# Second projection of a two-layer attention and SwiGLU kernel: order of chunk 2's turn and load, place of the block-diagonal keys, form of one closing down step

## The chip, the cores and the metric

The kernel runs on one core of one Trainium2 chip. The metric is the device time of one execution in microseconds (us). The engines are named as in the profile: PE (TensorE, matrix products), DVE (VectorE), ACT (ScalarE), POOL (GpSimd) and SP (SyncE, which here issues the transfers). PEld is the weight load of PE.

## The reference

Two equal layers over 2048 tokens of 448 features: attention with 16 query heads of 28 and one shared key and value head, then a SwiGLU feed-forward with 1792 inner features. Both are added to the residual, and both see a layer-normed input.

```python
for layer in range(2):          # the reference writes the two out
    h = layernorm(x)
    q = (h @ wq).heads(16)      # 28 wide each
    k, v = h @ wk, h @ wv       # one head for all
    p = softmax(q @ k.T * 28 ** -0.5)
    x = x + (p @ v).merged() @ wo
    h = layernorm(x)
    x = x + (silu(h @ w_gate) * (h @ w_up)) @ w_down
```

## The kernel before

Tokens are worked in four chunks of 512 (`c` = 0 to 3), each of four tiles of 128 rows. Every factor of a product is split into a high and a low part, and a product is the sum of three matmul passes: high by high, high by low, low by high. The residual `xres` stays in SBUF, and each engine runs its instructions in the order in which the program emits them; nothing is reordered. Transfers go through SP's queue in that same order. Tiles from a pool with a fixed number of buffers are handed out again as soon as the last reader is done; which buffer is taken is decided when the program is built.

**Feed-forward.** `unit(gi, c, n)` works one block of 128 inner features (`fc`) on one chunk: gate and up products, the activation on ACT and DVE, its split `hh`, `hl`. The down product of a unit is deferred: `down` (L861) returns it as two steps, which the next unit runs between and behind its own products. Inner blocks go in groups of two (`groups`), the four chunks inside a group. In half rows the partitions 0 to 63 and 64 to 127 work as two independent halves on two of the four down banks each; the second step swaps the pairs. Between the two steps `between` (L339) lets ACT copy one column of each bank (`seen`), so that the halves don't add to one bank at once. `by_tile` (L894) does the same sum with all 128 rows, one bank after the other, and needs no such look; it is used for the second layer's last chunk and for the very first unit of a layer. `accumulate` (L903) then adds the four banks to `xres`: tiles 0 and 1 on DVE (L911), tiles 2 and 3 by an ACT copy into a tile of the `stage` pool (two buffers, L914) and a POOL addition (L915).

**Hand-over.** After the last group of layer 0, `hand_over(c)` (L929) prepares chunk `c` for the second attention's projection: statistics on DVE (L216, L217), the reciprocal deviation on POOL (L223, L224), then for chunks 0 to 2 the steps `turn` (apply the norm on DVE, L230; turn 32x32 squares on DVE, L271; send the result to DRAM in four transfers, L277), `load` (four transfers back into the free query tiles `qstack`, L964 to L967) and `parts` (split: ACT copies L295 and L299, DVE subtractions L296 and L305). They are queued on `self.soon` with a count of units; `unit` counts down and runs what is due, in list order. For chunks 0 and 1 `load` is part of `turn`. For chunk 2 it stands in the projection's plan, and chunk 3 is turned by PE instead (`flip`, L251).

**Projection.** `project` (L499) does one of 16 steps, four per chunk. A step has an entry `plan[n, 0]` ahead of its matmuls and `plan[n, 1]` and `when[n]` behind them. `q` (L521) is its product (L315): 11 matmuls, an ACT cast and an ACT copy of the result (L548, L549), its output to DRAM (`qd`, L550; parts of the keys, `kt`, L553), and for the two steps of a chunk that carry values a DVE transposition (L556) and POOL copies (L559). Steps 0 to 3 put the copy into the same `stage` tiles. `first_keys` (step 2, L408) loads eight keys; `diagonal` (step 3, L412) makes the block-diagonal key tile `kdiag` from them on DVE; `maxima`, behind steps 6, 10 and 14, multiplies it with the queries (L441) and reduces (L443 to L456).

In the last two units of layer 0 (chunk 3, `fc` 12 and 13) and behind them the emitted order is: step 0 and 1; the last unit; then what is due on `self.soon`, in the order of chunk 1's `parts`, step 2, chunk 2's `turn`; step 3; the last down step, its adds and chunk 3's statistics; steps 4 to 15.

Of the kernel before, what the change touches and what calls it, by code (L numbers as in the profile page):

```python
# [23 lines left out]
NC = S // 512  # L24
NG = H // 4
NF = F // P
# [29 lines left out]
def forward(  # L56
# [31 lines left out]
    phase, banks, threes, live, turn = ExitStack(), [], [], set(), {}  # L88
# [114 lines left out]
    def xtile(pool, again=None):  # L203

        return (
            pool.tile([P, 4, 512], F32R, name="xh"),
            pool.tile([P, 3, 512], F32R, name="xl"),
            again,
        )

    def norm_steps(c, pool=pers, twice=True, each=False):

        got = {}

        def stat(t):
            nc.vector.bn_stats(stats[:, 4 * c + t, :], xres[:, 4 * c + t, :])  # L216
            nc.vector.bn_aggr(mv[:, 4 * c + t, :], stats[:, 4 * c + t, :])  # L217

        def scale(t0=0, n=4):
            if "r" not in got:  # L220
                got["r"] = pers.tile([P, 4], F32, name="rstd", bufs=2)
            r = got["r"][:, t0 : t0 + n]
            nc.gpsimd.tensor_scalar(r, mv[:, 4 * c + t0 : 4 * c + t0 + n, 1], 1.0, EPS, ALU.mult, ALU.add)  # L223
            nc.gpsimd.tensor_tensor(r, r, halfn[:, 0:n], ALU.pow)  # L224

        def apply(t):
            if t == 0:
                got["x"] = pool.tile([P, 4, 512], F32, name="xn")
            o, i, r = got["x"][:, t, 0:D], xres[:, 4 * c + t, :], got["r"][:, t : t + 1]
            nc.vector.tensor_scalar(o, i, mv[:, 4 * c + t, 0:1], r, ALU.subtract, ALU.mult)  # L230
            if twice:
                nc.gpsimd.tensor_copy(got["x"][:, t, D:512], o[:, 384:D])

        if each:
            fs = [lambda t=t: (stat(t), scale(t, 1)) for t in range(4)] + [lambda: None]
        else:
            fs = [lambda t=t: stat(t) for t in range(4)] + [scale]
        return fs + [lambda t=t: apply(t) for t in range(4)], got
# [30 lines left out]
    def turn_tile(got, tb, t):  # L269

        nc.vector.transpose(tb[:, :, 32 * t : 32 * t + 32], got["x"][:, t, 0:D].rearrange("p (b w) -> p b w", w=32))  # L271

    def send(tb, raw):

        to = raw.rearrange("(b d) (g n) -> g d b n", d=32, g=4)
        for g in range(4):
            nc.sync.dma_start(to[g], tb[32 * g : 32 * g + 32])  # L277
# [52 lines left out]
    def side_by_side(lower, upper):  # L330

        assert len(lower) == len(upper)
        for two in zip(lower, upper):
            for po, (a, b), start, stop in two:
                nc.tensor.matmul(po, a, b, start=start, stop=stop, skip_group_check=True)  # L335
# [3 lines left out]
    def between(*pos):  # L339

        for i, po in enumerate(pos):
            nc.scalar.copy(seen[:, i : i + 1], po[:, 0:1])  # L342
# [3 lines left out]
    class Attention:  # L346


        def __init__(self, layer):
            self.layer = layer  # L350
            self.squares = (0, 1, 2) if layer else ()
            self.X, self.norms, self.qd = {}, {}, {}
            self.done, self.spare = 0, {}
            self.order = [(c, m) for c in range(NC) for m in (TURN if c < NC - 1 else LAST)]
            self.seen = 0
            self.steps, self.places = [], []
            self.lent, self.plan = None, {}
            self.hi, self.rowsof, self.kt, self.when = {}, {}, {}, {}
            for c in range(NC):
                self.kt[c] = dram.tile([32, 512], F32, name=f"kt{layer}_{c}")  # L360
                self.at(4 * c + 4, lambda c=c: self.key_load(c))
                self.at(4 * c + 7, lambda c=c: self.key_split(c))
            for i in range(3):
                self.at(4 + 3 * i, lambda i=i: self.stack(i))
                self.at(6 + 3 * i, lambda i=i: self.parts(i))
                if not full:
                    self.at((9, 11, 13)[i], lambda i=i: self.rows(i))
            if not full:
                self.at(2, self.first_keys)
                self.at(3, self.diagonal)  # L370
            for i in range(len(GR) if full else 0):
                fs, place = self.max_steps(i)
                if i == 1:
                    fs[KC] = lambda f=fs[KC]: (f(), self.places[0]())
                self.steps += fs
                self.places.append(place)
# [475 lines left out]
    groups = [range(f, min(f + FG, NF)) for f in range(0, NF, FG)]  # L852

    class FeedForward:
# [6 lines left out]
        def down(self, fs, fc, d, hh, hl):  # L861


            _, _, dh, dl = self.W[fc]
            if self.layer == 1 and d is self.dn.get(NC - 1) and fs is groups[-1]:
                return [lambda: self.by_tile(fs, fc, d, ((hh, dh), (hh, dl), (hl, dh))), lambda: None]
            if fc == 0 and d is self.dn[0]:
                return [lambda: self.by_tile(fs, fc, d, ((hh, dh), (hh, dl), (hl, dh))), lambda: None]
            self.flip = 1 - self.flip
            one, two = ((0, 1), (2, 3)) if self.flip else ((2, 3), (0, 1))  # L870

            def step(ts, first):
                lists = []
                for upper, half in enumerate(ts):
                    rs = slice(64 * upper, 64 * upper + 64)
                    lists.append(
                        [
                            (
                                d[t][:, 0:D],
                                (a[rs, P * t : P * t + P], b[rs, :]),  # L880
                                first and fc == fs[0] and z == 0,
                                not first and fc == fs[-1] and z == 2,
                            )
                            for t in half
                            for z, (a, b) in enumerate(((hh, dh), (hh, dl), (hl, dh)))
                        ]
                    )
                side_by_side(*lists)
                if first:
                    between(*d)  # L890

            return [lambda: step((one, two), True), lambda: step((two, one), False)]
# [36 lines left out]
        def hand_over(self, c):  # L929

            a = self.nxt
            fs, got = norm_steps(c, twice=c == NC - 1)
            for f in fs[:5]:
                f()
            a.pool = self.stage

            if c == NC - 1:

                def ready():
                    for f in fs[5:]:  # L940
                        f()
                    a.norms[c] = got

                a.X[c] = xtile(self.xbp)
                a.plan[5, 1] = [ready]
                return
            to = dram.tile([D, 512], F32, name=f"xt1_{c}")
            raw = [q.bitcast(F32)[:, z, :] for q in qts[1:] for z in range(2)]

            def turn():  # L950
                for f in fs[5:]:
                    f()
                pool = (xpool, self.x1p, self.xbp)
                tb = pool[min(c + 1, 2)].tile([P, 4, 512], F32R, name="xh").bitcast(F32)
                tb = tb.rearrange("p a (b n) -> p (a b) n", n=P)[:, 0 : D // 32, :]
                for t in range(4):
                    turn_tile(got, tb, t)
                send(tb, to)
                a.X[c] = xtile(pool[c])
                if c < 2:  # L960
                    load()

            def load():
                nc.sync.dma_start(qts[1].bitcast(F32), to[0:256, :].rearrange("(k p) n -> p k n", p=P))  # L964
                nc.sync.dma_start(raw[2], to[256:384, :])
                for half in (slice(0, 64), slice(64, 128)):
                    nc.sync.dma_start(raw[3][half, :], to[384:448, :])  # L967

            def parts():
                halved(a.X[c], raw, range(4), nc.scalar.copy, nc.vector.tensor_tensor)  # L970

            self.soon.append([1, turn])
            if c == 2:
                a.plan[4, 1] = [load]
                a.plan[7, 0] = [parts]
                return
            self.soon.append([3, parts])
            self.soon.append([4 - c, lambda: [a.project() for _ in range(2 - c)]])
# [164 lines left out]
    fs, got = norm_steps(0)  # L1143
# [23 lines left out]
    for c in range(1, NC):  # L1167
        fs, got = norm_steps(c)
# [39 lines left out]
```

## Time and profile before

| | us |
|---|---|
| median of 3 runs | 1944.67 (1944.64 to 1945.7) |
| profiled execution, device time | 1948.05 |
| its span, first to last instruction | 1946.3 |
| PE busy in the span | 1933.1 |
| DVE, ACT, POOL busy | 978.1, 1256.8, 563.8 |
| mean granted clock of PE | 0.998 |

The second projection lies at about 966 to 1028 us of the span. Lines of a timeline give the start, the duration, engine, line and operation, what is written and read, how many instructions are merged, and in brackets the idle time of the engine ahead of it with the one that ended it. PE's matmuls overlap: a new one starts about every 0.2 us, though each lasts about 0.4.

### The profile page before, as it was taken

To read this page: it belongs to the slowest core of one execution; us is meant where nothing else is said; L and a number is where in the kernel's file an instruction comes from. 1 tells how busy PE (TensorE), PEld (TensorE's weight loads), DVE (VectorE), ACT (ScalarE), POOL (GpSimd) and SP (SyncE) were. 2 spreads that over 40 slices of the span, in tenths; PEclk is the share of its full clock that TensorE was granted. 3 is DMA by queue.
4 is the path that set the end of the run, shared out by engine and by line. 5 is a ranking of instruction groups with operands and counts; after the bars stand their busy time and mean duration, and the time that the engine had idled before them with its cause. 6 is when DMAs were issued, how large, how long until landed. Compare 5 with 4: busy or idle time off the path is not lost. (4 is left out here: it accounts for less than half of the span.)

```text
span 1946.3 us, 43775 instructions
## 1 busy us (share of the span) xinstructions
PE 1933.1 (99%) x18369; PEld 1325.7 (68%) x18369; DVE 978.1 (50%) x1675; ACT 1256.8 (65%) x1863; POOL 563.8 (29%) x608
## 2 busy tenths in 40 slices
PE   9999999999999999999999999999999999999998
PEld 7544544445469999999974445454454799988887
DVE  6655575665754322322665565657656532232223
ACT  4799899898953333333359998989989433333332
POOL 4213123122215333432342221122231352333420
PEclk9999999999999999999999999999999999999999
DMA  5211011021122011100251110110211220011102
GB/s 160 63 33 33 20 32 50 23 54 33 35 81 73 17 33 32 32 19 25 60 156 48 34 34 18 43 38 26 53 52 30 81 61 26 17 32 32 33 2 77
DMA packets 105474, 87.52 MB, mean 45 GB/s; under 512 B 25304, under 2 KB 85464, under 8 KB 105272
## 3 DMA queue, kind: packets, MB, share of 16 engines
q1 hardware_dynamic: 103576, 83.25, 15.4%
q8 instruction: 144, 2.36, 0.5%
q10 hardware_dynamic: 1696, 1.43, 0.2%
q14 instruction: 58, 0.48, 0.1%
HBM read 59.48 MB, written 23.33 MB: 43 GB/s over the span
## 5 line engine op out<-in xcount | busy, mean ns | idle before, releaser
L669 ACT ACTIVATE pt<-three 128x1536 f32<-128x1536 f32 x512 | 722.1, 1478 | 52.9 <-PE three L643 52.8
L703 PE MATMUL bank<-pt,vsb 128*32 128x512 f32 x3072 | 490.8, 598 | 0.6 <-ACT pt L669 0.6
L703 PE MATMUL bank<-pair,vsb 128*32 128x512 f32 x1024 | 487.7, 598 | 0.0
L643 PE MATMUL bank<-qstack,keys 32*128 32x512 f32 x1536 | 472.7, 425 | 0.0
L335 PE MATMUL bank<-xh,wgh 64*128 64x512 f32 x1712 | 439.0, 389 | 0.4 <-ACT seen L342 0.4
L643 PE MATMUL three<-qstack,keys 32*128 32x512 f32 x4608 | 429.0, 408 | 0.5 <-ACT stage L549 0.3
L643 PEld LDWEIGHTS bank<-qstack,keys 32*128 32x128 f32 x1536 | 243.2, 183 | 248.1 <-issue 125.4
L666 DVE COPY pair<-bank 128x512 f32<-128x512 f32 x512 | 353.9, 691 | 96.5 <-PE bank L643 65.6
L335 PE MATMUL bank<-xh,wgl 64*128 64x512 f32 x1391 | 363.8, 390 | 0.0
L335 PE MATMUL bank<-xl,wgh 64*128 64x512 f32 x1284 | 329.5, 389 | 0.0
L1035 DVE TENSOR_TENSOR sg<-bank,sg 128x512 f32<-128x512 f32 x112 | 77.3, 690 | 486.8 <-ACT sg L1034 476.3
L335 PE MATMUL bank<-wdh,h 64*128 64x448 f32 x1728 | 320.8, 363 | 0.8 <-DVE h L1041 0.4
L671 ACT ACTIVATE pair<-pair 128x1024 f32<-128x1024 f32 x254 | 277.6, 1093 | 0.0
L643 PEld LDWEIGHTS three<-qstack,keys 32*128 32x128 f32 x4608 | 262.0, 183 | 14.2 <-DVE xres L614 1.5
L703 PEld LDWEIGHTS bank<-pt,vsb 128*32 128x32 f32 x3072 | 101.7, 109 | 249.2 <-issue 153.2
L335 PEld LDWEIGHTS bank<-xh,wgh 64*128 64x128 f32 x1712 | 260.9, 184 | 15.2 <-issue 1.0
L915 POOL TENSOR_TENSOR xres<-stage,xres 128x448 f32<-128x448 f32 x107 | 126.1, 1197 | 479.9 <-ACT stage L914 479.7
L711 DVE TENSOR_TENSOR o<-bank,o 128x512 f32<-128x512 f32 x224 | 154.7, 691 | 202.1 <-PE bank L703 202.0
L335 PEld LDWEIGHTS bank<-wdh,h 64*128 64x128 f32 x1728 | 238.4, 184 | 12.4 <-DVE h L1041 1.2
L342 ACT COPY seen<-bank 128x1 f32<-128x1 f32 x646 | 79.4, 163 | 244.7 <-PE bank L335 242.0
L335 PEld LDWEIGHTS bank<-xh,wgl 64*128 64x128 f32 x1391 | 214.9, 184 | 12.6
L335 PE MATMUL bank<-wdl,h 64*128 64x448 f32 x864 | 212.0, 366 | 0.0
(150 smaller groups left out, 2133.2 us busy)
## 6 DMA issues: line engine op xcount, KB each, us to landing
o<-rd SPq DMA_DIRECT2D x32, 256.0 KB
qraw<-qd SPq DMA_DIRECT2D x128, 56.0 KB
xt<-tb SPq DMA_DIRECT2D x32, 224.0 KB
wdr<-in_B_w_down_dram SPq DMA_DIRECT2D x28, 224.0 KB
xn<-xt SPq DMA_DIRECT2D x8, 768.0 KB
wr<-in_B_w_gate_dram SPq DMA_DIRECT2D x28, 192.0 KB
wr<-in_B_w_up_dram SPq DMA_DIRECT2D x28, 192.0 KB
qd<-stage SPq DMA_DIRECT2D x20, 224.0 KB
```

The source lines that it names most:

```text
L335: nc.tensor.matmul(po, a, b, start=start, stop=stop, skip_group_check=True)
L342: nc.scalar.copy(seen[:, i : i + 1], po[:, 0:1])
L643: nc.tensor.matmul(three[:, j, :] if j < 3 else one, k[js, kp, ks], q[js, part, :], start=(z == 0), stop=(z == 2), tile_position=(32 * j, 0),)
L666: copies.append(nc.vector.tensor_copy(pt1, one))
L669: es.append(nc.scalar.activation(pt, threes[y], AF.Exp, scale=SCALE))
L671: es.append(nc.scalar.activation(pair, pair, AF.Exp, scale=SCALE))
L703: nc.tensor.matmul(to[32 * j : 32 * j + 32, :], vsb[:, n % NT, :], pts[n][j], start=(y == 0), stop=(y == 1), skip_group_check=True,)
L711: f = nc.vector.tensor_tensor(accs[i][:, 0, :], to, accs[i][:, 0, :], ALU.add)
L915: nc.gpsimd.tensor_tensor(r, s, r, ALU.add)
L1035: nc.vector.tensor_tensor(in_order(sg, True), natural(pg[1], True), in_order(sg, True), ALU.mult)
```

## The change

Four edits, all around the hand-over to the second projection.

1. `diagonal` runs behind step 4 instead of step 3 in the second layer.
2. The down step of the last chunk and the last inner block is done by `by_tile` in the first layer too. The block ahead of it keeps its half rows.
3. Chunk 2's `turn` is put at the head of `self.soon`, so that it runs ahead of chunk 1's `parts` and of step 2, all in the same unit.
4. Chunk 2's `load` is issued ahead of step 4's matmuls, not behind them.

```diff
             if not full:
                 self.at(2, self.first_keys)
-                self.at(3, self.diagonal)
+                self.at(4 if layer else 3, self.diagonal)
...
             _, _, dh, dl = self.W[fc]
-            if self.layer == 1 and d is self.dn.get(NC - 1) and fs is groups[-1]:
+            if d is self.dn.get(NC - 1) and fs is groups[-1] and (self.layer == 1 or fc == NF - 1):
                 return [lambda: self.by_tile(fs, fc, d, ((hh, dh), (hh, dl), (hl, dh))), lambda: None]
...
-            self.soon.append([1, turn])
+            self.soon.insert(0 if c == 2 else len(self.soon), [1, turn])
             if c == 2:
-                a.plan[4, 1] = [load]
+                a.plan[4, 0] = [load]
                 a.plan[7, 0] = [parts]
                 return
             self.soon.append([3, parts])
```

## The prediction

> **What bounds the kernel now.** I read the page's busy shares, then the stages of the second projection, then each engine's timeline there. On the page TensorE (PE) is the bound:
>
> ```profile
> span 1946.3 us, 43775 instructions
> PE 1933.1 (99%) x18369; PEld 1325.7 (68%) x18369; DVE 978.1 (50%) x1675; ACT 1256.8 (65%) x1863; POOL 563.8 (29%) x608
> ```
>
> Only 13.2 us of the span are free of PE work. The busy times by stage (columns: stretch, length, then busy us and instructions of PE, PEld, DVE, ACT, POOL, then clock, DMA share, GB/s) show what of it lies where the edits are:
>
> ```profile
> 980.00:1000.00 20.00, 19.64 (x110) 15.46 (x107) 15.11 (x30) 11.07 (x24) 6.71 (x14) 1.00 0.47 127
> 1000.00:1100.00 100.00, 98.81 (x914) 53.93 (x916) 61.29 (x108) 85.63 (x87) 27.45 (x48) 1.00 0.23 69
> ```
>
> That is 0.36 and 1.19 us. Where edits touch 1.55 us of idle PE, and matmuls are neither added nor removed in column count, a gain above 0.2% (3.9 us) is out of reach; 0.2% is also about what a measurement of this kernel tells from no change. The question is which of these stalls goes and which new one comes. PE's timeline (start, duration, idle before and its releaser):
>
> ```profile
> 987.30 0.39 PE L315 MATMUL bank<-xh,wl 128*128 128x512 f32 x1
> ...
> 989.48 0.47 PE L335 MATMUL bank<-wdh,h 64*128 64x448 f32 x2 [0.36 <-ACT seen L342]
> ...
> 990.90 0.50 PE L315 MATMUL bank<-xh,wh 128*128 128x512 f32 x1
> ...
> 998.53 1.10 PE L441 MATMUL bank<-q,kdiag 112*128 112x512 f32 x4
> ...
> 1001.98 1.91 PE L251 MATMUL bank<-ident,xn 128*128 128x128 f32 x16
> 1004.60 0.50 PE L315 MATMUL bank<-xh,wh 128*128 128x512 f32 x1 [0.71 <-ACT xh L295]
> ...
> 1007.29 0.50 PE L315 MATMUL bank<-xh,wh 128*128 128x512 f32 x1
> ```
>
> Three stations: the closing down step in half rows from 987.5 to 990.9 with a wait for the ACT look at its banks; the block-diagonal product at 998.53, unhindered; and step 8, the first on chunk 2, at 1004.60, which waits for its split and is through at its last block at 1007.29. Behind that PE runs on without a stall for 20 us. So the time changes by what that 1007.29 changes.
>
> **The change, part by part.** *Closing down step in full rows.* The second layer's last chunk runs such a step already and shows the pace:
>
> ```profile
> 1936.14 0.37 PE L898 MATMUL bank<-wdh,h 128*128 128x448 f32 x1
> 1936.34 0.37 PE L898 MATMUL bank<-wdl,h 128*128 128x448 f32 x1
> 1936.55 0.57 PE L898 MATMUL bank<-wdh,h 128*128 128x448 f32 x2
> ```
>
> 0.205 us each, twelve of them 2.46 us, plus the 0.23 us of the projection matmul ahead: step 4 would begin at 987.30 + 0.23 + 2.46 = 990.0 instead of 990.90. PE is 0.9 us ahead there, the four looks that ACT takes at the banks and their handshake fall away. It is kept only if nothing behind it is late.
>
> *Chunk 2 turned sooner.* The same eight DVE instructions move ahead of the four subtractions that split chunk 1 and ahead of step 2. DVE's timeline:
>
> ```profile
> 983.89 1.89 DVE L296 TENSOR_TENSOR xl<-qstack,xh 128x512 fp32r<-128x512 f32 x3
> ...
> 986.53 0.72 DVE L556 STREAM_TRANSPOSE vt<-bank 32x512 f32<-32x512 f32 x1
> 987.28 1.85 DVE L230 TENSOR_SCALAR xn<-xres,mv,rstd 128x448 f32<-128x448 f32 x4
> ...
> 991.30 0.72 DVE L556 STREAM_TRANSPOSE vt<-bank 32x512 f32<-32x512 f32 x1
> 992.05 0.69 DVE L412 TENSOR_TENSOR kdiag<-few,mask 112x512 fp32r<-112x512 f32 x1
> 992.77 1.16 DVE L911 TENSOR_TENSOR xres<-bank,xres 128x448 f32<-128x448 f32 x2
> 993.85 0.62 DVE L216 BATCH_NORM_STATS2 stats<-xres 128x6 f32<-128x448 f32 x1
> ...
> 996.69 0.63 DVE L216 BATCH_NORM_STATS2 stats<-xres 128x6 f32<-128x448 f32 x1 [0.55 <-POOL xres L915]
> ...
> 998.95 1.78 DVE L230 TENSOR_SCALAR xn<-xres,mv,rstd 128x448 f32<-128x448 f32 x4 [1.42 <-POOL rstd L224]
> 1000.65 0.71 DVE L443 STREAM_TRANSPOSE sg<-bank 128x512 f32<-128x512 f32 x1
> ...
> 1003.02 0.72 DVE L556 STREAM_TRANSPOSE vt<-bank 32x512 f32<-32x512 f32 x1
> 1004.58 1.94 DVE L296 TENSOR_TENSOR xl<-qstack,xh 128x512 fp32r<-128x512 f32 x3 [0.83 <-ACT xh L295]
> 1006.54 0.69 DVE L305 TENSOR_TENSOR xh<-qstack,xh 64x512 fp32r<-64x512 f32 x1
> ```
>
> The turn takes 991.30 - 987.28 = 4.02 us; moved to 983.89 it ends at 987.9. Chunk 1's split, 2.64 us (983.89 to 986.53), then ends at 990.6; step 4, from 990.0, wants its first low half 0.23 us later and that is ready at 988.6, its last one at 992.1: no wait, with 1.5 us to spare. DVE does the same work to 992.05, so its adds come no later by this.
>
> On SP's queue the four sends of the turned chunk are moved too, ahead of step 2's output and of the first-keys load:
>
> ```profile
> 970.44 3.01 SPq L277 DMA_DIRECT2D xt<-xh  x4
> 976.65 0.38 SPq L964 DMA_DIRECT2D qstack<-xt  x1
> ...
> 986.33 0.30 SPq L550 DMA_DIRECT2D qd<-stage  x1
> ...
> 991.29 3.00 SPq L277 DMA_DIRECT2D xt<-xh  x4
> 994.39 1.18 SPq L550 DMA_DIRECT2D qd<-stage  x1
> ...
> 998.85 0.39 SPq L964 DMA_DIRECT2D qstack<-xt  x1
> ```
>
> The sends go out at 987.9 instead of 991.29. Their landing is read from chunk 1: its load waits for them and goes out 976.65 - 970.44 = 6.21 us after the first send. Step 2's output, 986.33 before, now leaves behind four issues, at 987.9 + 3.1 = 991.0. It lies behind 4 x 224 KB; at a quarter of 6.21 us for 224 KB, 1.55 us, I estimate it landed at 987.9 + 6.21 + 1.55 = 995.65. The nearest row for a low end is the old place: ACT took that buffer again at 990.43 without waiting for it, at most 4.1 us after the issue, so 995.1 if the queue ahead costs nothing, and less is possible; the high end is the estimate slowed by traffic. I take 995.65, since the sends do lie ahead of it.
>
> Who waits for that output? The stage pool has two buffers, and both then hold outputs of steps 2 and 3. The ACT copy of down tile 2 takes one back:
>
> ```profile
> 990.43 0.53 ACT L914 COPY stage<-bank 128x448 f32<-128x448 f32 x1 [0.68 <-PE bank L335]
> 994.88 0.53 ACT L914 COPY stage<-bank 128x448 f32<-128x448 f32 x1 [3.92 <-POOL xres L915]
> ...
> 1003.93 1.82 ACT L295 CAST xh<-qstack 128x512 fp32r<-128x512 f32 x3 [3.65 <-DMA qstack<-xt]
> ```
>
> ```profile
> 993.69 1.16 POOL L915 TENSOR_TENSOR xres<-stage,xres 128x448 f32<-128x448 f32 x1
> 995.49 1.16 POOL L915 TENSOR_TENSOR xres<-stage,xres 128x448 f32<-128x448 f32 x1 [0.64 <-ACT stage L914]
> ```
>
> Before, the first copy was free at 990.43 and POOL came to it at 993.69, 3.3 us of slack. After, it waits to 995.65; copy to add is 0.61 us (994.88 to 995.49), so POOL's first add is at 996.3, 2.6 us late. The second add follows one add later at best, 997.45; if the second copy again waits for the first add's buffer, as at 994.88, it comes 1.80 us (993.69 to 995.49) later, 998.1. The other buffer should come free about 1 us behind the first, so I take 997.6. Behind the waiting copy on ACT stand the table load and the query copies of steps 4 to 6, which have PSUM banks to spare, and then chunk 2's casts.
>
> *Load of chunk 2 ahead of step 4.* It goes out when the sends have landed, 987.9 + 6.21 = 994.1 to 995.0, against 998.85 now: about 4 us sooner, which removes the wait for data behind 1004.60 and behind DVE's 0.83 us. Its cover is complete; the split is then limited by DVE alone.
>
> *Block-diagonal keys a step later.* The 0.69 us go from 992.05 to behind the last statistics of chunk 3. DVE's adds start 0.72 us sooner, worth nothing since the last statistics wait for POOL. The last statistics stand 1.20 us (995.49 to 996.69) behind the second add: 998.8; their end and the keys are 0.86 + 0.72 us on: 1000.4. That lies in the 1.42 us in which DVE waits for POOL anyway, so it delays no DVE work; but PE wants it at 998.53 - 0.9 = 997.6. A new PE stall of about 2.8 us opens before the block-diagonal product, which eats the 0.9 us won.
>
> **The sum** along the chain that then ends last, DVE's: statistics 998.8, apply 2.26 us on (996.69 to 998.95) 1001.1, block-diagonal transposition 1.70 on 1002.8, value transposition 2.37 on 1005.1, chunk 2's subtractions 0.75 on 1005.9 (against 1004.58), and step 8's last block 2.71 behind that (1004.58 to 1007.29): 1008.6 against 1007.29. PE's own path asks less: product at 1000.4, step 8 after 5.2 us more (998.53 to 1004.60 less the 0.71 and a little start-up), 1005.6. So the profiled span grows by 1.3 us, to 1947.6. The profiled execution took 1948.05 us, 1.75 beside its span, and the median of the runs shown, 1944.67, lies 3.4 below it. The difference carries over: 1944.67 + 1.3 = 1946.0 us, 0.07% slower, no change by the 0.2% bound.
>
> **Rivals.** *The stage buffer comes free in time* (output landed before POOL's 993.7): POOL's adds stay, DVE's order stays, and the subtractions follow the value transposition at 1003.02 + 0.75 = 1003.8 instead of 1004.58: -0.8 us, 1943.9. For it: the output is one small transfer against a queue of 16 engines. Against it: it leaves at 991.0 and would have to land in 2.7 us through four transfers that took 6.21. The Trainium skill, "DMA: Bandwidth & Descriptors", section on the anatomy of one DMA, gives about 2.0 us plus bytes over 436 GB/s, some 2.5 us for this output as an estimate, which would make this rival the forecast at 1943.9; its section on queues, rings and completion order has descriptors consumed in ring order and a completion only after every earlier write, which speaks for mine. The 6.21 us of chunk 1's sends bear out the second, and no row yet shows an output behind them.
>
> *The whole saving shows*: if also the keys and statistics come early, PE keeps the 0.9 us and loses the 0.71 us wait at 1004.60: -1.6 us, 1943.1. Against it stands DVE, full from 983.89 to 998.
>
> *Slower beyond 0.2%*: the same buffer wait, with the output slowed by the transfers behind it (first keys, step 3's output, the load of chunk 2). It decides from 2.6 us beyond my estimate, 998.3, a landing 7.3 us after issue against my 4.65: then +3.9 us or more, 1948.6. For it: before, chunk 2's load took 1003.93 - 998.85 = 5.1 us to its first casts, in company. Against: that first piece is 512 KB, over twice this output.
>
> *It does not do what it says*: the load goes out no sooner, because SP stands behind step 3's output; then the cost is the 1.3 us or the old 1007.29, inside the range.
>
> **How the numbers follow.** Forecast 0.60 (own range 1945.0 to 1947.4, from a landing 1 us earlier or the serial copies and some traffic); buffer in time 0.25; whole saving 0.08; slower beyond 0.2% 0.05; others 0.02. The predicted time is the first's, 1946.0. The range 1943.6 to 1948.2 takes in the first rival and the slow half of the forecast and leaves the two outer ones. Faster by over 0.2% needs more than all stalls here: 0.02; slower 0.05; within 0.2% 0.93.
>
> **What would show it.** Right: twelve full-row matmuls between steps 3 and 4, no looks on ACT; sends at about 988; step 2's output at 991; the first stage copy of the last down step held by a DMA until about 995.6; the product at 1000.4 held by the keys; step 8's subtractions with no wait for data. Wrong: the copy at 990, no keys stall, or a stall of PE at chunk 1's low half near 990.

## The result and the profile after

| | before | after |
|---|---|---|
| median of 17 runs, us | 1944.77 (1943.5 to 1947.66) | 1947.98 (1946.41 to 1950.7) |
| ratio to before | | 1.0017, 95% interval 1.001 to 1.0024 |
| profiled execution, us | 1948.05 | 1946.97 |
| its span, us | 1946.3 | 1945.2 |

The changed kernel is 3.2 us slower (1.9 to 4.7 by the interval). That is 0.17%, inside the 0.2% bound though the interval's upper end of 0.24% lies past it, and clear of the noise of this comparison, which is finer than the 0.2% that the prediction took for its limit. The two profiled executions stand the other way round. The one of before was 3.3 us above its median; its first 50 us ran at a granted clock of 0.93 (the third number from the right), those of after at 1.00:

```profile
0.00:50.00 50.00, 45.16 (x214) 37.03 (x215) 33.00 (x72) 20.52 (x39) 23.22 (x63) 0.93 0.52 160
```

```profile
0.00:50.00 50.00, 44.95 (x231) 37.16 (x232) 35.14 (x75) 22.69 (x44) 25.40 (x67) 1.00 0.53 164
```

So spans are no measure here, and the stage has to be compared with itself. On the page of after and in its busy times by stage the lines that answer to those of before are these:

```profile
span 1945.2 us, 43740 instructions
PE 1930.2 (99%) x18357; PEld 1325.1 (68%) x18357; DVE 976.9 (50%) x1675; ACT 1255.9 (65%) x1859; POOL 564.2 (29%) x608
```

```profile
980.00:1000.00 20.00, 16.80 (x73) 13.64 (x72) 14.13 (x29) 10.26 (x20) 6.12 (x14) 0.96 0.48 136
1000.00:1100.00 100.00, 99.74 (x925) 55.13 (x923) 61.14 (x108) 85.49 (x86) 28.50 (x48) 0.99 0.21 59
```

PE's idle time around the second projection was 0.36 and 1.19 us in these two stretches; it is now 3.20 and 0.26 us, and the granted clock is no longer 1.00. As everything ahead lies about 3 us earlier in this execution, I count from the last matmul of step 3 to the first score matmul of the second attention, with the projection between them. PE's timeline after:

```profile
984.27 0.40 PE L315 MATMUL bank<-xh,wl 128*128 128x512 f32 x1
984.50 0.37 PE L898 MATMUL bank<-wdh,h 128*128 128x448 f32 x1
...
986.97 0.40 PE L315 MATMUL bank<-xh,wh 128*128 128x512 f32 x1
...
997.82 1.48 PE L441 MATMUL bank<-q,kdiag 112*128 112x512 f32 x4 [3.19 <-DVE kdiag L412]
...
1002.95 1.91 PE L251 MATMUL bank<-ident,xn 128*128 128x128 f32 x16
1004.62 0.47 PE L315 MATMUL bank<-xh,wh 128*128 128x512 f32 x1
...
1026.69 0.50 PE L643 MATMUL three<-qstack,keys 32*128 32x512 f32 x3
```

and the end of the same stretch in the kernel before:

```profile
1027.34 0.50 PE L643 MATMUL three<-qstack,keys 32*128 32x512 f32 x3
```

Before, the stretch is 1027.34 - 987.30 = 40.04 us; after, 1026.69 - 984.27 = 42.42 us: 2.4 us longer. The full-row step does its part: step 4 starts 2.70 us behind the last matmul instead of 3.60. Then PE stands 3.19 us for the block-diagonal keys. Step 8 (1004.62) no longer waits for chunk 2. Why the keys are late, on SP's queue, ACT, POOL and DVE in turn:

```profile
984.80 3.00 SPq L277 DMA_DIRECT2D xt<-xh  x4
987.89 1.13 SPq L550 DMA_DIRECT2D qd<-stage  x1
...
990.26 0.43 SPq L550 DMA_DIRECT2D qd<-stage  x1
992.15 0.38 SPq L964 DMA_DIRECT2D qstack<-xt  x1
```

```profile
992.70 0.54 ACT L914 COPY stage<-bank 128x448 f32<-128x448 f32 x1 [6.92 <-DMA qd<-stage]
994.57 0.53 ACT L914 COPY stage<-bank 128x448 f32<-128x448 f32 x1 [1.34 <-POOL xres L915]
```

```profile
993.38 1.16 POOL L915 TENSOR_TENSOR xres<-stage,xres 128x448 f32<-128x448 f32 x1 [3.13 <-ACT stage L914]
995.18 1.13 POOL L915 TENSOR_TENSOR xres<-stage,xres 128x448 f32<-128x448 f32 x1 [0.64 <-ACT stage L914]
997.28 0.54 POOL L223 TENSOR_SCALAR rstd<-mv 128x4 f32<-128x4 f32 x1 [0.96 <-DVE mv L217]
```

```profile
996.34 0.63 DVE L216 BATCH_NORM_STATS2 stats<-xres 128x6 f32<-128x448 f32 x1 [0.92 <-POOL xres L915]
997.00 0.18 DVE L217 BATCH_NORM_AGGREGATE mv<-stats 128x2 f32<-128x6 f32 x1
997.10 0.66 DVE L412 TENSOR_TENSOR kdiag<-few,mask 112x512 fp32r<-112x512 f32 x1
998.95 1.78 DVE L230 TENSOR_SCALAR xn<-xres,mv,rstd 128x448 f32<-128x448 f32 x4 [1.19 <-POOL rstd L224]
...
1003.76 1.98 DVE L296 TENSOR_TENSOR xl<-qstack,xh 128x512 fp32r<-128x512 f32 x3
```

Step 2's output leaves behind the four sends, ACT stands 6.92 us for the buffer that it holds, POOL for ACT, DVE's last statistics for POOL, and the keys stand behind those statistics. Chunk 2's load goes out at 992.15, 7.9 us behind step 3's last matmul instead of 11.5, and is not what ends last any more. The landings that the trace records agree: the four sends issued from 984.80 had all landed at 992.07, step 2's output, issued at 987.89, at 992.60, and ACT's copy starts at 992.70. In the kernel before, step 2's output was issued at 986.33 with no transfer still under way ahead of it and had landed at 988.56, 2.2 us later; now it takes 4.7.

### The profile page after: what moved, and what is told of

The parts are those of the page before. It is cut to its first block, busy times and chain, and to the rows that moved or that the text cites. A ratio compares the mean times of both kernels' runs of the same rounds, so it can differ in the third digit from the quotient of the medians.

```text
span 1945.2 us, 43740 instructions
## 1 busy us (share of the span) xinstructions
PE 1930.2 (99%) x18357; PEld 1325.1 (68%) x18357; DVE 976.9 (50%) x1675; ACT 1255.9 (65%) x1859; POOL 564.2 (29%) x608
## 5 line engine op out<-in xcount | busy, mean ns | idle before, releaser
L669 ACT ACTIVATE pt<-three 128x1536 f32<-128x1536 f32 x512 | 734.2, 1526 | 52.4 <-PE three L643 52.4
L671 ACT ACTIVATE pair<-pair 128x1024 f32<-128x1024 f32 x254 | 290.1, 1142 | 0.0
```

Source lines behind the costliest of these rows:

```text
L669: es.append(nc.scalar.activation(pt, threes[y], AF.Exp, scale=SCALE))
L671: es.append(nc.scalar.activation(pair, pair, AF.Exp, scale=SCALE))
```

## The experiments

Times are medians beside runs of the kernel before on the same chip; the stretch is the one above, in the profiled execution. The chips differ: before had a median of 1945.2 beside the first group (turn back, keys back, buffers free, no keys) and beside the third (after once more, sends behind step 2 and the two versions built on it), and of 1946.2 beside the second (PE kept busy, and the three edits alone).

| | ratio to before, 95% interval | stretch, us |
|---|---|---|
| before | 1 | 40.04 |
| after | 1.0017 (1.001 to 1.0024) | 42.42 |
| after, once more | 1.0016 (1.0007 to 1.0025) | 43.49 |
| after, turn back | 0.9993 (0.9984 to 1.0002) | 39.15 |
| after, keys back | 1.0012 (1.0003 to 1.0021) | 42.16 |
| after, buffers free | 0.9993 (0.9984 to 1.0002) | 38.64 |
| after, no keys | 1.0014 (1.0005 to 1.0023) | 42.45 |
| after, PE kept busy | 1.001 (1.0001 to 1.0019) | 42.36 |
| before, full rows alone | 1.0003 (0.9994 to 1.0012) | 39.32 |
| before, turn alone | 1.0012 (1.0003 to 1.0021) | 43.02 |
| before, keys alone | 0.9995 (0.9986 to 1.0004) | 39.88 |
| after, sends behind step 2 | 0.9995 (0.9986 to 1.0004) | 39.34 |
| the same, keys back, chunk 2 split sooner | 1.0012 (1.0003 to 1.0021) | 42.46 |
| the same, buffers free too | 1.0003 (0.9994 to 1.0012) | 40.08 |

Theory 1 is that of the prediction. Theory 2, its rival, puts the cost on the later place of the keys by itself.

**Turn back in its place, the rest as changed.**

```diff
-            self.soon.insert(0 if c == 2 else len(self.soon), [1, turn])
+            self.soon.append([1, turn])
```

> The changed kernel with chunk 2's turn put back to its old place, behind chunk 1's split and step 2; the other three edits stay. Theory 1 (step 2's output stands behind the turned chunk's sends, so its stage buffer, the last residual rows and with them the keys come late): the first stage copy of the last down step no longer waits for a DMA, the block-diagonal product waits less than 1 us for the keys, and the time falls back to 1944.0 to 1945.0 us. Theory 2 (the later place of the keys is the cause by itself): the product still waits about 3 us and the time stays at 1947 to 1949.

1944.05 us against 1945.2. ACT's first stage copy waits 0.8 us, and for PE instead of a DMA; its second waits 4.2 us for POOL, as before the change. PE's wait for the keys is gone, and what is left is a wait at step 8. The waits of PE in this kernel (what waited and for whom, total us, times, longest):

```profile
PE bank L315 <- DVE xl L296: 0.9, 1, 0.9
PE three L643 <- ACT xn L549: 0.3, 1, 0.3
```

The keys are in the later place here and cost nothing: theory 2 falls, and the turn's place is the cause. Against before the interval reaches 1.0002; against the changed kernel the difference is clear.

**Keys back behind step 3, the rest as changed.**

```diff
-                self.at(4 if layer else 3, self.diagonal)
+                self.at(3, self.diagonal)
```

> The changed kernel with the block-diagonal keys back behind step 3. Theory 1: the product's wait goes, but DVE now stands at the keys for the first-keys load, which still lies behind the sends, about 3.5 us ahead of its adds, and PE waits some 4 us at the chunk 3 transpositions instead; 1947 to 1949 us. Theory 2: the wait goes and nothing takes its place; 1943.9 to 1944.8 us.

1947.4 us, as theory 1 has it. The product does not wait, yet the stretch is as long; PE stands at chunk 3's transpositions instead:

```profile
PE bank L251 <- DVE sg L443: 3.1, 1, 3.1
```

The releaser is one that I had not expected: not the applied rows but the transposition of the block-diagonal product (L443), which follows them on DVE. In all six executions in which PE stood there (keys back, no keys, full rows alone, turn alone and the last two versions), it went on 0.05 to 0.06 us behind that transposition's end. That the two share a PSUM bank would explain it, but was not tried. So undoing the edit that shows in the trace as PE's wait brings nothing. The edit was the place where the lateness showed, not its source.

**Outputs of steps 2 and 3 in other buffers.**

```diff
-            elif self.layer and self.seen > 3:
+            elif self.layer and self.seen > 1:
```

> The changed kernel with the outputs of steps 2 and 3 held in the buffers that steps 4 and later use, so that the down step's copies find the stage buffers free. Theory 1: ACT's first copy comes about 2 to 5 us sooner, the product's wait shrinks below 0.5 us, DVE's chain ends 2.5 to 4 us sooner; about 1943.2 us (1942.5 to 1944.5). Theory 2: no difference to the changed kernel, 1947 to 1949 us.

1943.68 us against 1945.2, and the stretch is 38.64, 3.8 us less than the changed kernel's. Both stage copies come at once, at 2.28 and 2.90 us behind step 3's last matmul (8.43 and 10.30 in the changed kernel). The sends still lie ahead of step 2's output; only nobody waits for it. This shows the buffer to be the link, and this kernel has the shortest stretch of all and the lowest median of its group. Its interval reaches 1.0002, so that it beats before by 1.5 us is likely, not settled; against the changed kernel it is clear.

**No second-layer keys.**

```diff
-                self.at(4 if layer else 3, self.diagonal)
+                if not layer:
+                    self.at(3, self.diagonal)
```

> The changed kernel without the second layer's block-diagonal keys: that layer's bounds are taken with the first layer's keys, so the tile is there long before. Left out is this one multiplication. Theory 1: the product no longer waits, but chunk 3's statistics are as late as before and PE waits about 4 us at its transpositions; 1946.5 to 1948.5 us. Theory 2: about 1943.9 us. If the half clock behind the product's wait is worth 1 to 2 us and no wait of that length takes its place, 1946 to 1946.5 us.

1947.68 us; the product is not held, and PE stands 3.0 us at the transpositions. The late statistics alone carry the cost.

**PE kept busy in its wait.**

```diff
+            if self.layer and c == 0:
+                for _ in range(14):
+                    nc.tensor.matmul(pm, self.w[0][:, 0, 0:P], self.X[1][0][:, 0, :], start=True, stop=True)
```

> The changed kernel with 14 matmuls of 512 columns (about 3.2 us), whose sums nobody reads, on PE ahead of the first block-diagonal product, where it waited 3.19 us. Nothing else moves. If the half clock that the trace of the changed kernel shows behind that wait (3.41 us at 0.5) is what lies between my +1.3 us and the measured +3.2, the time falls to 1946.0 to 1946.7 and no half clock stands there. If DVE's chain sets the end in any case, only about 0.3 us comes back: 1947.5 to 1947.9, also without the half clock.

Between step 6 and the product this kernel has no idle PE, and its clock stays whole. The granted clock is the third number from the right; first the changed kernel, then the same kernel once more, then this one:

```profile
994.00:998.00 4.00, 0.81 (x4) 0.37 (x3) 2.19 (x5) 3.40 (x7) 2.31 (x4) 1.00 0.60 214
998.00:1002.00 4.00, 4.00 (x11) 3.12 (x12) 3.02 (x6) 3.71 (x8) 2.42 (x5) 0.57 0.49 138
1002.00:1006.00 4.00, 4.00 (x27) 3.54 (x26) 3.80 (x9) 2.85 (x6) 2.01 (x4) 1.00 0.62 187
```

```profile
994.00:998.00 4.00, 1.26 (x6) 0.72 (x4) 1.85 (x5) 2.81 (x5) 2.40 (x3) 0.94 0.71 256
998.00:1002.00 4.00, 3.60 (x9) 2.83 (x10) 2.77 (x7) 3.49 (x8) 2.92 (x6) 0.50 0.37 97
1002.00:1006.00 4.00, 4.00 (x21) 3.38 (x20) 3.83 (x8) 1.93 (x5) 1.47 (x3) 0.71 0.55 170
```

```profile
998.00:1002.00 4.00, 3.92 (x18) 2.92 (x17) 2.78 (x8) 3.94 (x9) 2.82 (x5) 1.00 0.41 76
```

Its stretch is 42.36 us, 0.06 less than the changed kernel's in the first execution: there the half clock lay under DVE's chain and cost next to nothing. In the second execution, for which 42.4 us had been expected, the half clock lasted twice as long and the stretch is 43.49, 1.1 us more. By run times, 1.0010 against 1.0016 and 1.0017, the intervals overlap; 2.2 us above before on its chip, this kernel lies between the two sizes expected (1.2 to 1.9 and 2.7 to 3.1 above the 1944.77 of before). So the half clock costs from 0 to about 1.1 us in these two executions, and DVE's chain 2.3 us without it.

**Full rows alone, turn alone, keys alone, on the kernel before.**

```diff
-            if self.layer == 1 and d is self.dn.get(NC - 1) and fs is groups[-1]:
+            if d is self.dn.get(NC - 1) and fs is groups[-1] and (self.layer == 1 or fc == NF - 1):
```

> The kernel before with the closing down step in full rows and nothing else. PE comes 0.9 us sooner to step 4. If step 8 still waits for chunk 2's load, the gain is lost there and PE's wait grows from 0.7 to about 1.6 us: 1944.6 to 1945.2 us against 1945.0 before. If the saving showed: about 1944.1.

```diff
-            self.soon.append([1, turn])
+            self.soon.insert(0 if c == 2 else len(self.soon), [1, turn])
```

> The kernel before with chunk 2's turn at the head and nothing else. Theory 1: the stage copy waits for step 2's output as in the changed kernel; the keys behind step 3 wait on DVE for the first-keys load behind the sends; the load of chunk 2, still behind step 4's outputs on SP, comes no sooner than before: 1947.5 to 1949.5 us. If the turn harmed nothing alone: 1944 to 1945.

```diff
-                self.at(3, self.diagonal)
+                self.at(4 if layer else 3, self.diagonal)
```

> The kernel before with the keys a step later and nothing else. Theory 1: the keys are ready at about 998.2 us of the span, PE asks for them at 998.5: no wait, 1944.7 to 1945.3 us, as before. Theory 2 (the later place is the cause by itself): a wait of 1 to 3 us and 1946.5 to 1948.5 us.

Full rows alone shorten the stretch by 0.7 us, more than I gave them: PE's waits behind do not grow to 1.6 us but come to 0.9 in all, as the load's first piece was split 0.8 us sooner in this execution. The run times don't tell this from nothing (0.9994 to 1.0012). The turn alone is slower, 1948.81 against 1946.2, within what was expected; its DVE shows the wait for the first-keys load, which now stands behind the sends, and ACT the one for the buffer again:

```profile
DVE kdiag L412 <- DMA few<-kt: 3.8, 1, 3.8
```

```profile
ACT stage L914 <- DMA qd<-stage: 5.7, 1, 5.7
```

The keys alone change nothing: theory 2 falls a second time. The fourth edit, the place of chunk 2's load, was not run by itself. Where the turn is early, the load left 7.88 us behind step 3's last matmul with it (keys back) and 14.01 us without it (turn alone), but these two also differ in the closing down step; where the turn is late, it left at 11.07 us with it (turn back) and 11.09 us without it (keys alone).

**Sends behind step 2, turn still early on DVE.**

```diff
-                send(tb, to)
+                self.tb = tb
+                if c < 2:
+                    send(tb, to)
...
+            if c == 2:
+                self.soon.append([1, lambda: send(self.tb, to)])
```

> The changed kernel with chunk 2 turned on DVE as early as there, but its four sends emitted behind step 2, so that step 2's output and the first-keys load go ahead of them on SP's queue. Theory 1, sharpened: it is the order of the queue alone, not DVE's: the stage copy finds its buffer, the product's wait falls under 0.5 us, first scores 38.9 to 39.6 us behind step 3's last matmul, 0.5 to 1.1 us faster than before. If DVE's earlier turn is the harm: 41 us or more, slower than before.

1944.32 us against 1945.19, stretch 39.34, the product's wait 0.2 us. DVE runs the turn as early as in the changed kernel, so it is the order on SP's queue and not DVE's that does the harm.

**Two further versions, for a faster kernel.** To the sends behind step 2, the keys back behind step 3 and

```diff
-                a.plan[7, 0] = [parts]
+                a.plan[6, 0] = [parts]
```

> The same as the run with the sends behind step 2, with the keys back behind step 3 and chunk 2's split ahead of step 6 instead of 7, so that DVE subtracts ahead of the block-diagonal reductions. If DVE's chain (statistics, apply, reductions, value transposition, subtractions) is what ends last in the stage, PE finds the split done at step 8: no wait there, first scores 37.4 to 38.3 us behind step 3's last matmul, 1.8 to 2.6 us faster than before. If PE's own path or the load ends last: 39 us, about 1 us faster.

and with the outputs in other buffers as above

> The same again with the outputs of steps 2 and 3 in the later steps' buffers. The last statistics come 0.5 to 1 us sooner, but PE reaches chunk 3's transpositions no sooner than before, so if PE is the bound there by then, nothing more is won: 37.4 to 38.3 us, equal to the run before it within 0.3 us. If the statistics still held PE: 0.5 us less.

Both miss: 1947.61 and 1945.39 us. The split is done early, as I wanted, but it now stands ahead of L443 on DVE, and PE's transpositions wait for that (3.2 and 2.5 us). DVE and POOL of the first of the two:

```profile
1000.08 1.89 DVE L296 TENSOR_TENSOR xl<-qstack,xh 128x512 fp32r<-128x512 f32 x3
1002.00 0.69 DVE L305 TENSOR_TENSOR xh<-qstack,xh 64x512 fp32r<-64x512 f32 x1
1002.72 0.72 DVE L443 STREAM_TRANSPOSE sg<-bank 128x512 f32<-128x512 f32 x1
```

```profile
998.96 3.83 POOL L232 COPY xn<-xn 128x64 f32<-128x64 f32 x4 [0.61 <-DVE xn L230]
```

I had taken the transpositions to need the applied rows alone. They also wait for L443, and the run with the keys back had shown it before I made these.

## Why the prediction was right, and where its size was off

The direction and the mechanism hold, and so does a change within 0.2%: 1946.0 us forecast, 0.07% slower, in a range of 1943.6 to 1948.2; 1947.98 measured, 0.17% slower. The size was not good: the measured time lies above the 1945.0 to 1947.4 us that the forecast gave as its own, and only 0.2 us inside the stated range. Counted from step 3's last matmul (987.30 before, 984.27 after), step by step:

- *Full rows.* Step 4 at 2.70 us as forecast, and the ACT looks gone. The 0.9 us was eaten by the next wait, as forecast.
- *Chunk 1's split behind the turn.* No PE wait for it.
- *Sends ahead of step 2's output.* The estimate of its landing from chunk 1's 6.21 us plus a quarter put the stage copy at 995.65 - 987.30 = 8.35 us; measured 992.70 - 984.27 = 8.43. The two runs that free the buffer or let the output go first bear out that this is the cause. That the number is right to 0.1 us is luck: the four sends took 7.27 us to land (984.80 to 992.07), not 6.21, and the output landed 0.53 us behind them, not 1.55, two errors of about 1 us that cancelled. The prediction says that no row yet shows an output behind such sends. The landing records of the trace of before do have one: step 3's output, issued at 994.39 behind the sends of 991.29, had landed at 998.89, 4.50 us from issue.
- *Second add.* The step of the prediction that took 997.6 for it, on the ground that "the other buffer should come free about 1 us behind the first", is off: the second copy again reused the first add's buffer, and the adds stand 1.80 us apart, not 1.3. That is 0.5 us, in the direction of the bound named there.
- *Statistics to apply.* Forecast 2.26 us as before, measured 998.95 - 996.34 = 2.61. The statement that the keys' multiplication "delays no DVE work" is wrong by the 0.35 us in POOL's first small instruction, 0.54 instead of 0.20, which runs beside it and which DVE then waits for.
- *Keys.* Ready at 13.5 us behind step 3's last matmul against 13.1 forecast; PE's wait 3.19 us against 2.8.
- *End of the chain.* Chunk 2's subtractions at 1003.76 - 984.27 = 19.49 us against 17.28 before: 2.2 later, where the sum had 1.3. The two terms above, 0.5 and 0.35, are the difference.
- *Not in the sum at all.* PE's half clock behind the new wait. I had PE's path from the product to step 8 at 5.2 us; it took 6.8. It hides under DVE's chain in one execution and adds about 1.1 us in another. This is the term that was left at nothing.

So 2.2 to 2.4 us come from the chain and 0 to 1.1 from the clock; with both the measured 3.2 (1.9 to 4.7) is met. That the clock makes the spread of the run times, 1946.4 to 1950.7, is argued and not shown for each. What is on record is the mean granted clock of all 17 executions: 0.999 in seven with a median of 1946.97 us, 0.998 in seven with 1947.95, 0.997 in three with 1949.2, where 3.41 us at half clock take 0.0009 from the mean. But that mean takes in the opening of the kernel too, where before has such stretches as well.

Of the rivals, the buffer in time did not happen, but the three runs that bring it about (0.9993, 0.9993, 0.9995) have medians 0.9 to 1.5 us below before, about its 0.8 and more, though each interval reaches 1. The slow one past 0.2% did not happen either; the landing took 4.7 us from issue, 987.89 to 992.60, against 4.65 estimated. The Trainium skill's ring order ("DMA: Bandwidth & Descriptors", section on queues, rings and completion order) agrees with this output, which landed 0.53 us behind the last of the sends ahead of it. The Trainium skill's fixed cost plus bytes, some 2.5 us by the estimate in the prediction (same title, section on the anatomy of one DMA), is given there for one transfer issued from GpSimd, while these leave from SP; it is near the 2.2 us of the output that had the queue to itself, and not what an output behind four others takes.

## What to carry to other kernels

When a step is moved ahead on one engine, write down what its transfers pass on the issuing queue, and which small buffers those later transfers hold: an output that leaves late keeps its buffer, and the next writer of that buffer stands in its engine's line with all that is behind it. The wait that the trace shows on the bounding engine need not be undone where it shows; here undoing it moved the wait to the next product, and freeing the buffer or ordering the queue removed it. Estimate a landing from transfers that stood in the same place of the queue: here 4.5 us for an output behind four sends in the kernel before, and 4.7 us in the changed one. What the sum had missed were the buffer of a second copy, a small instruction slowed beside another engine, and the clock behind the new wait.

## What the runs showed of the hardware that was not expected

**Half clock behind a short wait.** At or behind PE waits of 2.06 to 3.19 us at the second projection the granted clock fell to 0.50 for 3.4 us, or 6.8 in one execution, in six executions of this study (the changed kernel twice, keys back, no keys, turn alone, split sooner); a wait of 2.49 us there (the last version) and all waits under 1 us left it whole. The opening of the kernel, which no edit touches, does the same: behind waits of 2.11 to 2.43 us in its first 15 us the clock was halved for 6.8 us in the profiled execution of before and for 3.4 us in three others (keys back, full rows alone, keys alone), while a wait of 2.58 us (split sooner) and waits of 1.65 to 1.80 us left it whole. Matmuls of 512 columns then start 0.43 us apart instead of 0.23. The Trainium skill ("TensorE: Matmul & The Clock Gate", section on HAM oscillation) asks for no idle gaps over about 3.4 us; here waits shorter than that were enough, and the measurement decides. In all 14 traces two changes of the clock lie a whole number of 3.41 us apart (993.28 us, or 291 of them, between two changes in the changed kernel). The Trainium skill's free-running window of about 3.4 us (same title, section "What's actually happening") fits this, and that the same wait cost 3.41 us of half clock in one execution and 6.83 in another.

**POOL slowed by DVE beside it.** POOL's instruction on 128x4 elements took 0.54 us wherever DVE made the keys at that time, and 0.19 to 0.20 in all kernels where it did not:

```profile
995.09 0.54 POOL L223 TENSOR_SCALAR rstd<-mv 128x4 f32<-128x4 f32 x1 [0.97 <-DVE mv L217]
```

is the kernel before with the keys alone moved. In the changed kernel it ended at 997.82, 0.06 us behind the keys' multiplication (997.10 to 997.76). POOL's four copies (L232) took 3.83 us beside DVE's subtractions of chunk 2 in the last two versions, and 1.51 elsewhere. The Trainium skill ("GPSIMD Engine Reference", section on specifications) has POOL share its SBUF interfaces with VectorE, with contention where a VectorE instruction has two SBUF inputs, as both of these have; the trace agrees.
